# Transposing q by the DMA crossbar instead of by TensorE, from the third batch on

## Chip, cores, metric

One NeuronCore of a Trainium2 chip (trn2). The metric is device time in microseconds of one execution; the kernel before takes 306.1 us.

The profiler's names: PE is TensorE at its matmuls and PEld its weight loads, DVE is VectorE, ACT ScalarE, POOL GpSimd, and SP SyncE, from whose queue (SPq) most DMAs are issued. A crossbar transpose is a DMA that transposes on its way. A transfer lands when its data are there and its semaphore says so. A product or transfer is due when everything ahead of it on its engine is done.

## The reference

Linear attention without softmax, a norm over each head, then a dense layer pair with a quick GELU between.

```python
kv  = np.einsum('bhsd,bhse->bhde', k, v)           # 8 batches, 8 heads, 576 rows, 64 wide
out = np.einsum('bhsd,bhde->bhse', q, kv)
rms = np.sqrt(np.mean(out * out, axis=-1, keepdims=True) + 1e-06)
x   = (out / rms * g_norm)                          # then (b, h, s, d) -> (b s, h d), 4608 x 512
h   = x @ w_in                                      # 512 -> 2048
g   = h * (1.0 / (1.0 + np.exp(-1.702 * h)))
y   = g @ w_out                                     # 2048 -> 512
```

## The kernel before

It runs nine dense layers (one per batch of 512 rows, and a last one for the 8 x 64 rest rows). The attention of batch t + 1 is threaded between the matmuls of layer t. The matmul of this kernel for `out = q kv` takes q with the head dimension on the partitions, so q has to be transposed. The first two batches get this from a matmul with a stacked identity. From the third batch on it is done so:

```python
def q(self, c):                                   # c: pair of heads, 4 per batch
    t = ps_a.tile([P, SM + P], F16, name="qTp", tag="att")
    for j in range(J):                            # 4 transposes of 128x128
        nc.tensor.transpose(t[:, j * P : (j + 1) * P], qh[:, c, j, :], ident)
    n = SM
    if c >= 2:                                    # the rest rows of two pairs
        nc.tensor.transpose(t[:, SM : SM + P], qrem[self.b % 2][:, c - 2, :], ident)
        n += P
    s = attn.tile([P, SM + P], F16, name="qT", tag="qT", bufs=6)
    nc.vector.tensor_copy(s[:, 0:n], t[:, 0:n])   # PSUM to SBUF
    self.qT[c] = s
```

`casts(b)` makes the fp16 copies of k, q and v on DVE, in the order k, q, v for pair 0, then pair 1, and so on. The layers schedule these units by position: `at1(i, ...)` after the i-th of 16 hidden tiles of a layer, `at2(n, ...)` after the n-th of its 64 output matmuls, both counted from 0.

```python
            at1(f0, casts, b)                     # f0 = 7 in the second layer, else 2
            at1(f0, start, b)
            for c in range(NPAIR):
                at1((11 if t == 1 else 8) + c, of(b, "kv", c))
                at1(12 + c, of(b, "q", c))
            for c in range(NPAIR + 1):
                at2(1 + 9 * c, of(b, "out", c))   # first product after output matmul 1
# ... cut
            if b + 2 < B:
                at2(2, load_batch, b + 2)         # and load_batch(3) at the end of the first layer
```

All outputs, the loads of k, q and v from the third batch on and (after the change) the transposes are issued from SP, in program order.

Of the kernel before, what the change touches and what calls it, by code (L numbers as in the profile page):

```python
# [8 lines left out]
F16 = mybir.dt.float16  # L9
# [4 lines left out]
P = 128  # L14
# [3 lines left out]
def kernel(  # L18
# [10 lines left out]
    nc = tc.nc  # L29
# [4 lines left out]
    NPAIR = H // 2  # L34
# [3 lines left out]
    SM = 512  # L38
    J = SM // P
    R = S - SM  # L40
# [7 lines left out]
    attn = ctx.enter_context(tc.tile_pool(name="attn", bufs=4))  # L48
# [3 lines left out]
    ps_a = ctx.enter_context(tc.tile_pool(name="ps_a", bufs=3, space=bass.MemoryType.PSUM))  # L52
# [11 lines left out]
    qrem = [const.tile([P, 2, P], F16, name=f"qrem{i}") for i in range(2)]  # L64
    kbuf = const.tile([P, NPAIR * NJ * P], F16)
    qbuf = const.tile([P, NPAIR * NJ * P], F16)
    vbuf = const.tile([P, NPAIR * NJ * D], F16)
    ident = const.tile([P, P], F16)
# [39 lines left out]
    qh = qbuf[:, 0 : NPAIR * SM].rearrange("p (c j e) -> p c j e", c=NPAIR, j=J)  # L108
# [82 lines left out]
    class Attention:  # L191
# [21 lines left out]
                    r = slice(hl * D, (hl + 1) * D)  # L213
                    nc.vector.tensor_copy(self.kb[r, :, r], t[r, :, r])  # L214

        def q(self, c):
            t = ps_a.tile([P, SM + P], F16, name="qTp", tag="att")
            for j in range(J):
                nc.tensor.transpose(t[:, j * P : (j + 1) * P], qh[:, c, j, :], ident)  # L219
            n = SM  # L220
            if c >= 2:
                nc.tensor.transpose(t[:, SM : SM + P], qrem[self.b % 2][:, c - 2, :], ident)  # L222
                n += P
            s = attn.tile([P, SM + P], F16, name="qT", tag="qT", bufs=6)
            nc.vector.tensor_copy(s[:, 0:n], t[:, 0:n])  # L225
            self.qT[c] = s

        def rest(self, c):
            return self.qT[c | 2][:, SM + (c // 2) * R : SM + (c // 2 + 1) * R]

        def out(self, c):
            t = ps_a.tile([P, NPAIR, P], F32, name="outT", tag="att")
# [52 lines left out]
    class Early(Attention):  # L285
# [17 lines left out]
        def q(self, c):  # L303
            t = ps_h.tile([P, SM], F32, name="q9", tag="hT")
            for j in range(NJ - 1):
                nc.tensor.matmul(
                    t[:, j * R : (j + 1) * R], qz[:, c, j, :], stack, start=True, stop=True
                )
            s = attn.tile([P, SM + P], F16, name="qT", tag="qT", bufs=6)
            nc.vector.tensor_copy(s[:, 0:SM], t)  # L310
            self.qT[c] = s

        def q_rest(self):
# [169 lines left out]
    for t in range(NT):  # L483
        b = t + 1
        u1, u2 = {}, {}

        def at1(i, f, *args):
            u1.setdefault(i, []).append(lambda: f(*args))

        def at2(i, f, *args):  # L490
            u2.setdefault(i, []).append(lambda: f(*args))

        def of(b, name, *args):
            return lambda: getattr(live[b], name)(*args)

        if t == 0:
            at1(("ko", 1), of(0, "ss", NPAIR - 1))
            at1(("ko", 1), of(0, "apply", NPAIR - 1))
            at1(4, of(0, "q_rest"))
            at1(6, of(0, "out", NPAIR))  # L500
            at2(4, of(0, "ss", NPAIR, True))
            at2(4, of(0, "apply", NPAIR))
            at1(8, start, 1)
            for r in krem + vrem:
                at1(8, nc.vector.memset, r[R:P], 0.0)
            for c in range(NPAIR):
                s0 = 14 + 9 * c
                at2(s0 - 6, second_casts, c)
                at2(s0, of(1, "kv", c))
                at2(s0 + 2, of(1, "q", c))  # L510
                at2(s0 + 8, of(1, "out", c))
                at2(s0 + 13, of(1, "ss", c))
                at2(s0 + 13, of(1, "apply", c))
            at2(s0, third)
            at2(63, load_batch, 3)
        elif b < B:
            if t == 1:
                at1(3, of(1, "q_rest"))
                at2(46, of(1, "out", NPAIR))
                at2(53, of(1, "ss", NPAIR))  # L520
                at2(53, of(1, "apply", NPAIR))
            f0 = 7 if t == 1 else 2
            at1(f0, casts, b)
            at1(f0, start, b)
            for c in range(NPAIR):
                at1((11 if t == 1 else 8) + c, of(b, "kv", c))
                at1(12 + c, of(b, "q", c))
            for c in range(NPAIR + 1):
                at2(1 + 9 * c, of(b, "out", c))
                at2(8 + 9 * c, of(b, "ss", c, c == 0))  # L530
                at2(8 + 9 * c, of(b, "apply", c))
            if b + 2 < B:
                at2(2, load_batch, b + 2)
        dense(t, u1, u2, 4 if t < 2 else 0, t == 0)
# [30 lines left out]
```

## Time and profile before

| | before |
|---|---|
| time, median of 3 | 306.1 us (306.08 to 306.12) |
| span of the profiled run | 304.5 us |
| PE busy | 291.9 us, 96% |
| a layer with attention (layers 3 to 7) | 31.8 us |
| a layer without | 27.6 us |

Read it from PE down: where PE has no gap, the length of each piece of PE work is its price. The prediction below shows the stages and the chain. What the q unit does can also be asked by its tile: in the kernel before, this is the view of all instructions that read or write the PSUM tile `qTp` (line, engine, operation, count, then min/median/max ns, and when):

```profile
L219 PE MATMUL qTp<-ident,qbuf x96: 219/219/219, 65.0 to 228.6; 128*128 128x128 f16 x96
L225 DVE COPY qT<-qTp x24: 409/458/493, 65.5 to 228.9; 128x512 f16<-128x512 f16 x12, 128x640 f16<-128x640 f16 x12
L222 PE MATMUL qTp<-ident,qrem x12: 219/219/219, 67.9 to 228.6; 128*128 128x128 f16 x12
```

96 + 12 = 108 transposes and 24 copies are what the change takes away.

### The profile page before, as it was taken

The numbers are of one execution on the slowest core, as the hardware profiler recorded it, in microseconds if no ns is written. First come the engines' busy times: TensorE is split into PE (matmuls) and PEld (weight loads), VectorE is DVE, ScalarE is ACT, GpSimd is POOL, SyncE is SP. The second block draws the span as 40 slices with busy tenths as digits, with TensorE's granted clock in tenths as the row PEclk, the third lists the DMA queues.
The fourth block names the chain that finished last, engine by engine and source line by source line (L and its number), as shares of the span: only waits on it lengthen the run. The fifth ranks groups of instructions, "written<-read, shape, count | busy, mean of one in ns | idle before, by whom it ended". The sixth has DMA issues, their size and how long they took to land.

```text
span 304.5 us, 4193 instructions
## 1 busy us (share of the span) xinstructions
PE 291.9 (96%) x1657; PEld 140.9 (46%) x1657; DVE 108.8 (36%) x225; ACT 183.7 (60%) x293; POOL 29.6 (10%) x52
## 2 busy tenths in 40 slices
PE   6789989999999999999999999999999999999994
PEld 2334454454445544554455444544454444444441
DVE  5651066273461347124523444324523400110021
ACT  7588667757675775667466756585657756007400
POOL 5640070021030100010001000000000000000000
PEclk9999999999999999999999999999999999999999
DMA  6999995999999703870289003000300030002033
GB/s 154 288 176 197 253 262 191 298 334 252 331 237 308 196 0 138 286 182 0 85 276 247 1 0 138 2 0 2 138 0 0 3 138 0 2 15 123 2 69 69
DMA packets 38325, 41.04 MB, mean 135 GB/s; under 512 B 10913, under 2 KB 33441, under 8 KB 37537
## 3 DMA queue, kind: packets, MB, share of 16 engines
q1 hardware_dynamic: 33376, 35.39, 38.8%
q0 software_dynamic: 4768, 5.37, 10.8%
q8 instruction: 13, 0.21, 0.3%
q14 instruction: 8, 0.06, 0.1%
q10 hardware_dynamic: 160, 0.00, 0.0%
HBM read 36.70 MB, written 9.44 MB: 152 GB/s over the span
## 4 chain that ended last, share of the span: by engine, by line
PE 86%; DMA 10%; POOL 1%; SPq 1%; issue 0%; DVE 0%; POOLq 0%
PE o L370 40%; PE hT L329 36%; DMA w_out_sb<-in_moe_w_out_dram 5%; DMA qf<-in_q_dram 3%; PE ss L262 2%; PE outT L234 2%; PE kvp L202 2%; PE qTp L219 2%; DMA kf<-in_k_dram 2%; SPq L93 1%; PE kvp L210 0%; POOL qbuf L101 0%; POOL kbuf L101 0%; PE kv L290 0%; POOL w_in_sb L177 0%
## 5 line engine op out<-in xcount | busy, mean ns | idle before, releaser
L370 PE MATMUL o<-w_out_sb,gT 128*128 128x512 f16 x576 | 137.9, 379 | 0.0
L338 ACT ACTIVATE gT<-hT 128x512 f16<-128x512 f32 x142 | 84.4, 598 | 74.0 <-PE hT L329 73.7
L329 PE MATMUL hT<-xT,w_in_sb 128*128 128x512 f16 x504 | 118.0, 379 | 0.6 <-DVE xT L272 0.5
L370 PEld LDWEIGHTS <-gT 128*128 128x128 f16 x576 | 55.1, 98 | 62.8 <-issue 1.4
L329 PEld LDWEIGHTS <-w_in_sb 128*128 128x128 f16 x576 | 54.5, 98 | 59.8 <-issue 2.2
L378 DVE COPY osb<-o 128x512 f32<-128x512 f32 x34 | 23.3, 684 | 60.8 <-PE o L370 60.8
L272 DVE SCALAR_TENSOR_TENSOR xT<-outT,g_col,rs 128x512 f16<-128x512 f32 x32 | 24.0, 750 | 49.4 <-ACT rs L266 49.4
L264 ACT ACTIVATE ln<-ss,eps_t 128x512 f32<-128x512 f32 (+1 forms) x40 | 25.8, 645 | 18.6 <-PE ss L262 18.5
L266 ACT ACTIVATE rs<-ln 128x512 f32<-128x512 f32 (+1 forms) x40 | 23.5, 587 | 1.3
L254 ACT ACTIVATE sq<-outT 128x512 f16<-128x512 f32 (+1 forms) x40 | 21.6, 541 | 2.7 <-PE outT L234 2.7
L214 DVE CAST kvb<-kvp 64x256 f16<-64x256 f32 x12 | 5.1, 421 | 33.9 <-PE kvp L210 33.8
L145 POOL CAST krem<-krf 64x512 f16<-64x512 f32 x6 | 5.2, 863 | 110.1 <-DMA krf<-in_k_dram 110.1
L225 DVE COPY qT<-qTp 128x512 f16<-128x512 f16 (+1 forms) x24 | 11.0, 457 | 13.4 <-PE qTp L222 8.0
L262 PE MATMUL ss<-sq,ones 128*128 128x512 f16 (+1 forms) x40 | 14.3, 357 | 0.8 <-ACT sq L254 0.6
L329 PE MATMUL hT<-x_rem,w_in_sb 128*128 128x512 f16 x64 | 14.0, 379 | 0.0
L234 PE MATMUL outT<-qT,kvb 128*128 128x512 f16 x32 | 12.1, 379 | 0.5 <-DVE qT L310 0.3
L139 DVE CAST qbuf<-qf 128x512 f16<-128x512 f32 x24 | 10.5, 436 | 2.9 <-DMA qf<-in_q_dram 2.9
L143 DVE CAST vbuf<-vf 128x512 f16<-128x512 f32 x24 | 10.4, 435 | 0.0
L338 ACT ACT_TABLE_LOAD x8 | 10.3, 1283 | 0.1
L276 DVE SCALAR_TENSOR_TENSOR x_rem<-outT,g_col,rs 128x256 f16<-128x256 f32 x8 | 3.9, 483 | 17.9 <-ACT rs L266 17.9
L139 DVE CAST kbuf<-kf 128x512 f16<-128x512 f32 x24 | 10.2, 426 | 0.0
L422 PE MATMUL idle<-kvb 128*128 128x512 f16 x29 | 8.9, 436 | 1.2 <-DVE kvb L160 1.2
(57 smaller groups left out, 142.0 us busy)
## 6 DMA issues: line engine op xcount, KB each, us to landing
kf<-in_k_dram SPq DMA_DIRECT2D x6, 1024.0 KB, 6.8
vf<-in_v_dram SPq DMA_DIRECT2D x6, 1024.0 KB, 10.0
qf<-in_q_dram SPq DMA_DIRECT2D x6, 1024.0 KB, 12.3
out_dram<-osb SPq DMA_DIRECT2D x6, 1024.0 KB, 3.9
kf<-in_k_dram SPq DMA_DIRECT2D x8, 288.0 KB, 6.3
qf<-in_q_dram SPq DMA_DIRECT2D x8, 288.0 KB, 6.1
out_dram<-osb SPq DMA_DIRECT2D x4, 512.0 KB, 5.6
w_in_sb<-in_moe_w_in_dram POOLq DMA_DIRECT2D x2, 512.0 KB, 6.8
```

The source lines that it names most:

```text
L139: nc.vector.tensor_copy(out=dst[:, c, :, :].rearrange("p j (l d) -> p j l d", l=2), in_=src[n][:, h, :].rearrange("p l (j d) -> p j l d", ...
L225: nc.vector.tensor_copy(s[:, 0:n], t[:, 0:n])
L234: nc.tensor.matmul(t.rearrange("p c r -> p (c r)"), self.kb[:, c, :], self.qT[c][:, 0:SM], start=True, stop=True,)
L254: nc.scalar.activation(sq[:, 0:n], t, AFT.Square)
L262: nc.tensor.matmul(t[:, 0:n], ones2, sq[:, 0:n], start=True, stop=True)
L264: nc.scalar.activation(ln[:, 0:n], t[:, 0:n], AFT.Ln, bias=eps_t, scale=1.0 / D)
L266: nc.scalar.activation(rs[:, 0:n], ln[:, 0:n], AFT.Exp, bias=0.0, scale=-0.5)
L272: nc.vector.scalar_tensor_tensor(self.x[:, c, :], o, g_col, rs, op0=ALU.mult, op1=ALU.mult)
L329: nc.tensor.matmul(h, w_in_sb[:, ko, fo * P : (fo + 1) * P], x[:, ko, :], start=(ko == 0), stop=(ko == KO - 1),)
L338: nc.scalar.activation(gT[:, fo, :], h, AFT.Gelu_apprx_sigmoid)
L370: nc.tensor.matmul(os[mo], gT[:, fo, mo * P : (mo + 1) * P], w_out_sb[:, fo, :], start=(fo == 0), stop=(fo == FO - 1),)
L378: (nc.scalar.copy if deep and mo % 2 else nc.vector.tensor_copy)(osb[:, mo, :], os[mo])
```

## The change

Its intent is to take work off PE, which bounds the kernel, and give it to the DMA engines, which stand idle for much of a late layer.

```diff
-        def q(self, c):
-            ...                                   # as above: 4 or 5 TensorE transposes, one PSUM copy
+        def transpose_q(self):
+            s = attn.tile([P, NPAIR * J, P], F16, name="qTd", tag="qTd", bufs=1)
+            nc.sync.dma_start_transpose(out=s, in_=qbuf[:, 0 : NPAIR * SM])
+            self.qTr = attn.tile([P, 2, P], F16, name="qTr", tag="qTr", bufs=1)
+            nc.sync.dma_start_transpose(
+                out=self.qTr, in_=qrem[self.b % 2].rearrange("p c e -> p (c e)")
+            )
+            s = s.rearrange("p (c j) r -> p c (j r)", c=NPAIR)
+            for c in range(NPAIR):
+                self.qT[c] = s[:, c, :]
@@ schedule
-            at2(63, load_batch, 3)                # first layer
             at1(f0, casts, b)
             at1(f0, start, b)
+            at1(f0, of(b, "transpose_q"))
+            if t == 1:
+                at1(f0, load_batch, 3)
             for c in range(NPAIR):
                 at1((11 if t == 1 else 8) + c, of(b, "kv", c))
-                at1(12 + c, of(b, "q", c))
```

(The tile of the first two batches loses its unused tail and two of its six buffers; `rest` reads the new tile.)

More of the change, by code (lines that the diff above doesn't have):

```diff
@@ L214, in kv @@
                     nc.vector.tensor_copy(self.kb[r, :, r], t[r, :, r])
-        def q(self, c):
-            t = ps_a.tile([P, SM + P], F16, name="qTp", tag="att")
-            for j in range(J):
-                nc.tensor.transpose(t[:, j * P : (j + 1) * P], qh[:, c, j, :], ident)
-            n = SM
-            if c >= 2:
-                nc.tensor.transpose(t[:, SM : SM + P], qrem[self.b % 2][:, c - 2, :], ident)
-                n += P
-            s = attn.tile([P, SM + P], F16, name="qT", tag="qT", bufs=6)
-            nc.vector.tensor_copy(s[:, 0:n], t[:, 0:n])
-            self.qT[c] = s
+        def transpose_q(self):
[8 more added lines that the diff above has]
+                self.qT[c] = s[:, c, :]
         def rest(self, c):
-            return self.qT[c | 2][:, SM + (c // 2) * R : SM + (c // 2 + 1) * R]
+            return self.qTr[:, c % 2, (c // 2) * R : (c // 2 + 1) * R]
         def out(self, c):
@@ L308, in q @@
                 )
-            s = attn.tile([P, SM + P], F16, name="qT", tag="qT", bufs=6)
-            nc.vector.tensor_copy(s[:, 0:SM], t)
+            s = attn.tile([P, SM], F16, name="qT", tag="qT", bufs=4)
+            nc.vector.tensor_copy(s, t)
             self.qT[c] = s
```

## The prediction

> **What bounds the kernel now.** I read the page first (busy shares, then the chain that ended last), then the table by stage, then the timeline around the work that the change removes, then the timeline of the DMA queue's own engine.
>
> From the page, the busy shares and the head of the chain:
>
> ```profile
> PE 291.9 (96%) x1657; PEld 140.9 (46%) x1657; DVE 108.8 (36%) x225; ACT 183.7 (60%) x293; POOL 29.6 (10%) x52
> ...
> PE 86%; DMA 10%; POOL 1%; SPq 1%; issue 0%; DVE 0%; POOLq 0%
> ```
>
> PE is busy 96% of the span and makes 86% of the chain; the 10% of DMA lies in the first 38 us, which the change does not touch. From 53 us on, the program is one dense layer per batch, of some 31.8 us, with the attention of the next batch threaded in. The table by stage (PE, PEld, DVE, ACT, POOL busy, then clock, DMA share, GB/s) shows one such layer, from 85.5 us, and one that carries no attention, from 244.6 us:
>
> ```profile
> 85.50:117.30 31.80, 31.80 (x180) 15.62 (x179) 12.66 (x27) 20.91 (x34) 4.37 (x6) 1.00 0.62 158
> ...
> 244.60:272.20 27.60, 27.60 (x130) 12.48 (x129) 2.77 (x4) 9.55 (x16) 0.00 (x0) 1.00 0.10 39
> ```
>
> PE has no gap in either, at clock 1.00. So the price of a piece of PE work is its full length, and all of one batch's attention costs 31.8 - 27.6 = 4.2 us. DVE and ACT have slack.
>
> The q part of that, in the list of the chain in order of time (start, length, what), for the third layer:
>
> ```profile
> 98.03 0.22 PE qTp L219 x4
> 98.25 0.86 PE hT L329 x4
> 99.12 0.22 PE qTp L219 x4
> 99.34 0.86 PE hT L329 x4
> 100.20 0.22 PE qTp L219 x4
> 100.48 0.86 PE hT L329 x4
> 101.35 0.22 PE qTp L219 x4
> 101.62 0.43 PE o L370 x2
> ```
>
> Four transposes take 0.22 us, some 55 ns each in the stream, though one record lasts 219 ns. The third and fourth groups hold a fifth transpose (the rest rows), and take 0.28 and 0.27 us to the next start.
>
> **What the Trainium skill says.** (1) "VectorE: DVE Perf Modes", section The three transpose paths: a 128x128 transpose is 390 ns on TensorE and 1309 ns through the DMA crossbar. The trace agrees that a TensorE transpose is cheap and goes further: in the pipelined stream it costs 55 ns. (2) "Advanced Engine Details and Errata", section X-Bar Transpose (TRN2): crossbar transposes are as fast as regular DMAs, 350 to 400 GB/s expected. (3) "DMA: Bandwidth & Descriptors", section Latency and other measured facts: 261 GB/s measured for a transpose in one kernel. The trace of the kernel before has no transposing DMA, so it confirms neither; its plain loads move about 300 GB/s. (4) The same page, section Queues, rings and completion order: each DMA engine consumes the descriptors of one ring in ring order. The trace fits it: loads issued behind others land later (the 1 MB k, v and q loads of a batch take a median of 6.8, 10.0 and 12.3 us to land, though they are alike).
>
> **The change, part by part.**
>
> Removed from PE: per batch 4 x 4 + 2 = 18 transposes, 0.22 + 0.22 + 0.28 + 0.27 = 0.99 us of the path. Six batches (the third to the eighth): 6 x 0.99 = 5.9 us. All of it is on the path, since PE has no gaps. That is 1.9% of 306.1 us, so even a perfect result stops at 300.2 us, just short of 2%.
>
> Removed from DVE: 24 PSUM copies, the row reads 11.0 us at 457 ns. They lie beside PE work; worth nothing in time. PSUM buffers come free earlier; nothing waited for these.
>
> Added: per batch two DMAs on SP's queue, 128x2048 fp16 (512 KB) and 128x256 (64 KB). Both wait for the fp16 casts; the first product of the batch now waits for the whole big one. Its duration, issue to landing, is the disputed term; call it X. Estimates: 512 KB at the skill's 261 GB/s is 2.0 us, plus what a short DMA takes to land here, 2.3 us (the page's row of 128 KB outputs): 4.3 us. If 16 blocks of 128x128 ran one after another at 1.3 us it would be 21 us. I take X = 5 us, a little over the first[...].
>
> Moved: the load of the fourth batch. It was issued from 56.9 us on, ahead of everything; now it stands on SP behind the first transposes, which wait for the casts.
>
> The window for the transposes is not the same everywhere. In the second layer (first use), in the timeline:
>
> ```profile
> 64.81 0.41 DVE L139 CAST qbuf<-qf 128x512 f16<-128x512 f32 x1
> ...
> 69.64 0.10 PEld L234 LDWEIGHTS <-kvb 128*128 128x128 f16 x1
> ```
>
> The last q cast ends at 65.2; the first product starts at 69.6, or 68.7 once 0.99 us of transposes ahead of it is gone. Window W1 = 3.4 us. Stall S1 = X - 3.4 where positive.
>
> In the third layer the casts end early (about 90.1), but the queue is full. After the first transposes (end 65.3 + X) SP sends the fourth and fifth batches' loads, then the 1.1 MB output of the second layer, then the next transposes. A batch is 3.54 MB, at some 306 GB/s 11.6 us; the output 3.8 us. So those transposes land at 65.3 + X + 11.6 + 11.6 + 3.8 + X = 92.3 + 2X. The need is at 84.7 (layer start less 0.99) + S1 + 14.9 = 99.6 + S1, 14.9 being 100.5 - 85.6 from layer start to first product. Stall S2 = 92.3 + 2X - 99.6 - (X - 3.4) = X - 3.9.
>
> From the fourth layer on the queue is quiet when the casts end: in the timeline of SP the layer's own load starts only after them,
>
> ```profile
> 121.61 0.37 SPq L120 DMA_DIRECT2D kf<-in_k_dram  x1
> 122.28 0.37 SPq L120 DMA_DIRECT2D vf<-in_v_dram  x1
> ```
>
> and it now stands behind the transposes. Casts end 4.6 us after the layer's start, the need is at 14.9: window 10.3 us, no stall unless X is over that. The loads then start X later, but have a whole layer to land.
>
> Sum for X = 5: -5.9 + 1.6 + 1.1 = -3.2, so 302.9 us; I say 303.
>
> **The rivals.** A: the crossbar is as quick as plain DMA (X under 3.5). No stall anywhere, 300.2 us. For it: the skill's rate and the window of 3.4 us; against it: 2.3 us of fixed time leaves 1 us for 512 KB. B: it is about twice slower than I take (X = 8 to 10): S1 + S2 = 2X - 7.3, so 306.1 - 5.9 + 8.7 = 309 to 313 us: the wait on the transpose takes the place of the removed work, and only in two layers. For it: the 1309 ns of a single block, if only partly overlapped. C: blocks go one after another (X about 20): every layer waits, 4 x (20 - 10.3) more, near 370 us. D: the crossbar is not the matter, but the moved load of the fourth batch is: its casts wait at the third layer's start. By the sums above it lands near 65.3 + 5 + 11.6 = 82, before the casts at 86, so I hold it to be hidden unless X passes 9.
>
> **Range and chances.** The floor is 300.2 less a little, so "faster by over 2%" needs more than all the removed PE time: 0.06. X from 3.4 to 9.7 us covers 300.2 to 312.2, "same": 0.75. X above that, or a convoy in the queue: 0.19. The range, 299.8 to 314.0, is X from 0 to about 10.7.
>
> **What would show it.** In the profile after: PE's matmul count down by 108, with no qTp group; q transposes under DMA issues with their landing time, which is X; the first product waiting on that DMA in the second and third layers for about 1.6 and 1.1 us; the layers from the fourth on 30.8 us long instead of 31.8 with no PE idle time. Wrong if X is over 10 us (PE gaps at the first product in every layer), if the transposes hold up SP itself so that loads or outputs come late, or if other loads slow down beside a transpose.

## The result

The changed kernel took 301.24 us (median of 4 runs, 300.47 to 302.05), the kernel before 306.11 us beside it. Ratios here are the mean time of one kernel's fast runs over the mean of the other's fast runs of the same rounds, so they are not quite the ratio of the medians: 0.9841, with a 95% interval of 0.9806 to 0.9876. That is within 2%.

The busy shares and the head of the chain, page of the changed kernel:

```profile
PE 287.3 (96%) x1549; PEld 135.1 (45%) x1549; DVE 98.0 (33%) x201; ACT 184.0 (61%) x293; POOL 28.7 (10%) x52
...
PE 74%; DMA 18%; DVE 3%; POOL 1%; SPq 1%; issue 1%; ACT 0%; POOLq 0%; DVEq 0%
```

PE has 108 matmuls fewer and is 4.6 us less busy; DVE has 24 instructions and 10.8 us less. The chain now goes through DMA for 18% of the span, 8 points more: it passes through the load of the third batch, its casts and the first two transposes. From the chain in order of time (start, length, what):

```profile
49.13 11.93 DMA qf<-in_q_dram
...
65.66 4.39 DMA qTd<-qbuf
...
93.20 8.15 DMA qTd<-qbuf
```

The new operations, from the page's list of DMA issues (the last number is the median time to landing in us; the size of a transpose is not given):

```profile
qTd<-qbuf SPq DMA_TRANSPOSE x6, 4.4
qTr<-qrem SPq DMA_TRANSPOSE x6, 2.7
```

The fourth layer and the one without attention, table by stage:

```profile
117.00:147.81 30.81, 30.81 (x163) 14.65 (x161) 10.84 (x23) 20.64 (x33) 1.51 (x3) 1.00 0.59 169
...
240.23:267.85 27.62, 27.62 (x129) 12.54 (x128) 2.77 (x4) 9.57 (x16) 0.00 (x0) 1.00 0.09 39
```

The fourth to the seventh layer are each 1.0 us shorter and PE still has no gap there. The second and third layers are different. Timeline of the second layer (start, length, engine, what, idle before):

```profile
65.21 0.42 DVE L139 CAST qbuf<-qf 128x512 f16<-128x512 f32 x1
...
65.66 2.01 SPq L218 DMA_TRANSPOSE qTd<-qbuf  x1
...
69.21 0.59 PE L369 MATMUL o<-w_out_sb,gT 128*128 128x512 f16 x2
...
70.09 0.38 PE L233 MATMUL outT<-qTd,kvb 128*128 128x512 f16 x1 [0.29 <-DMA qTd<-qbuf]
```

The two output matmuls take 0.43 us, so the product was due at 69.64 and starts at 70.09: it waits 0.45 us (0.29 of it counted idle, as matmul ends are modelled). In the third layer:

```profile
93.20 6.00 SPq L218 DMA_TRANSPOSE qTd<-qbuf  x1
...
100.69 0.59 PE L369 MATMUL o<-w_out_sb,gT 128*128 128x512 f16 x2
101.40 0.38 PE L233 MATMUL outT<-qTd,kvb 128*128 128x512 f16 x1
```

This transpose is queued behind the fifth batch's load and the second layer's output. It lands 8.2 us after its issue (the longest of the six), and its product waits 0.28 us.

The whole account, from the starts of the layers in both traces: up to the second layer +0.78 us (0.72 of it is there when the first layer starts, as the first loads landed 0.7 us later in this run), second layer -0.55, third -0.72, fourth to seventh -4.01, the rest +0.26 (the last outputs land later). Sum -4.24: span 304.52 to 300.28 us.

### The profile page after: what moved, and what is told of

Its sections match the earlier page's. It is cut to its first block, busy times and chain, and to the rows that moved or that the text cites. A ratio compares the mean times of both kernels' runs of the same rounds, so it can differ in the third digit from the quotient of the medians.

```text
span 300.3 us, 3952 instructions
## 1 busy us (share of the span) xinstructions
PE 287.3 (96%) x1549; PEld 135.1 (45%) x1549; DVE 98.0 (33%) x201; ACT 184.0 (61%) x293; POOL 28.7 (10%) x52
## 4 chain that ended last, share of the span: by engine, by line
PE 74%; DMA 18%; DVE 3%; POOL 1%; SPq 1%; issue 1%; ACT 0%; POOLq 0%; DVEq 0%
PE o L369 37%; PE hT L328 30%; DMA qf<-in_q_dram 7%; DMA w_out_sb<-in_moe_w_out_dram 5%; DMA qTd<-qbuf 4%; PE ss L261 2%; DMA kf<-in_k_dram 2%; PE outT L233 2%; PE kvp L202 1%; SPq L93 1%; DVE qbuf L139 0%; DVE kbuf L139 0%; DVE kbuf L101 0%; DVE vbuf L143 0%; POOL kbuf L101 0%
## 5 line engine op out<-in xcount | busy, mean ns | idle before, releaser
L328 PE MATMUL hT<-xT,w_in_sb 128*128 128x512 f16 x504 | 115.5, 379 | 0.6 <-DVE xT L271 0.5
L328 PEld LDWEIGHTS <-w_in_sb 128*128 128x128 f16 x576 | 55.2, 98 | 63.3 <-issue 2.2
L261 PE MATMUL ss<-sq,ones 128*128 128x512 f16 (+1 forms) x40 | 14.3, 357 | 0.8 <-ACT sq L253 0.6
L145 POOL CAST krem<-krf 64x512 f16<-64x512 f32 x6 | 4.0, 659 | 112.8 <-DMA krf<-in_k_dram 89.4
L421 PE MATMUL idle<-kvb 128*128 128x512 f16 x29 | 10.1, 483 | 1.2 <-DVE kvb L160 1.2
L337 ACT ACT_TABLE_LOAD x8 | 10.3, 1283 | 0.1
L143 DVE CAST vbuf<-vf 128x512 f16<-128x512 f32 x24 | 10.3, 431 | 0.0
L202 PEld LDWEIGHTS <-kbuf 128*128 128x128 f16 x96 | 7.4, 98 | 5.7
L233 PE MATMUL outT<-qTd,kvb 128*128 128x512 f16 x24 | 9.1, 379 | 0.4 <-DMA qTd<-qbuf 0.3
```

Of the source, the lines that this page charges most:

```text
L202: nc.tensor.matmul(t[:, c, :].rearrange("p (l d) -> p l d", l=2), kh[:, c, j, :], vh[:, 2 * c : 2 * c + 2, j * D : (j + 1) * D], start=(j ...
L233: nc.tensor.matmul(t.rearrange("p c r -> p (c r)"), self.kb[:, c, :], self.qT[c][:, 0:SM], start=True, stop=True,)
L261: nc.tensor.matmul(t[:, 0:n], ones2, sq[:, 0:n], start=True, stop=True)
L328: nc.tensor.matmul(h, w_in_sb[:, ko, fo * P : (fo + 1) * P], x[:, ko, :], start=(ko == 0), stop=(ko == KO - 1),)
L337: nc.scalar.activation(gT[:, fo, :], h, AFT.Gelu_apprx_sigmoid)
```

## The experiments

**after_again: the changed kernel once more.** No edit.

> The changed kernel once more, to see whether its times really fall into two groups (300.5 and 302.0 us in the four runs so far, where the kernel before has 306.1 in all) and to get a second trace. Theory A (the two groups come from when the early loads land, before 48 us, and have nothing to do with the transposes): the layers from the fourth on last 30.8 us in any run, and the whole difference between two traces of different groups is there by the start of the second layer (54 us) or in the two first products that wait for a transpose. Theory B (the transposes themselves vary): some layer from the fourth on shows a wait at its first product.

300.66 us (300.51 to 301.31), ratio 0.9829. The profiled run took 300.70 us. In its second layer:

```profile
64.51 1.96 SPq L218 DMA_TRANSPOSE qTd<-qbuf  x1
...
68.34 0.59 PE L369 MATMUL o<-w_out_sb,gT 128*128 128x512 f16 x2
68.91 0.38 PE L233 MATMUL outT<-qTd,kvb 128*128 128x512 f16 x1
```

The product is due at 68.77 and waits 0.14 us; in the third layer 0.15. Layers four to seven take 30.8 us again. Against the first trace, the last copy of an output tile starts 1.33 us earlier: 0.86 of that is there at the start of the second layer, 0.31 and 0.13 are the two waits. So the spread has to do with what happens before 70 us, and with two waits, as theory A had it, except that these waits are for the transposes; no later layer varies. (What sets the longer wait is read from all traces together, at the end of this section.) That the times form two groups was an accident of four runs: with the later ones they fill the stretch from 300.5 to 302.8.

**no_transpose: products read the untransposed copy (wrong result).**

```diff
-            s = attn.tile(...); nc.sync.dma_start_transpose(...)   # both transposes
+            self.qTr = qrem[self.b % 2]
+            for c in range(NPAIR):
+                self.qT[c] = qbuf[:, c * SM : (c + 1) * SM]
```

> All transposes of q taken out: the products read the fp16 copy as it lies (wrong result on purpose). This is the floor: 306.1 - 5.9 = 300.2 us if the removed work is worth what the chain says and nothing else changes. If the two first waits of the changed kernel (0.4 and 0.3 us) are all that the crossbar costs, the changed kernel is 0.7 us above this one in runs with an equal start. If this one lies below 299.5 the crossbar costs more than its visible waits.

300.06 us (299.81 to 300.24), ratio 0.9805. The floor stands where the chain of the kernel before put it. In its trace the first product starts on time:

```profile
68.41 0.59 PE L363 MATMUL o<-w_out_sb,gT 128*128 128x512 f16 x2
68.84 0.38 PE L227 MATMUL outT<-qbuf,kvb 128*128 128x512 f16 x1
```

The changed kernel of the same call is 0.6 us above it. The profiled run of the changed kernel there (300.70 us) has 0.29 us of waits and is 0.46 us above the profiled run of this one (300.24 us). 0.25 us of that lie behind the last layer's start, where PE does the same work and the last outputs land later.

**move_only: the kernel before, with only the load of the fourth batch moved.**

```diff
-            at2(63, load_batch, 3)
             at1(f0, start, b)
+            if t == 1:
+                at1(f0, load_batch, 3)
```

> The kernel before, with only the load of the fourth batch moved behind the casts of the third, as in the changed kernel; q still transposed on TensorE. If the move is hidden (my step D): 306.1 us within 0.3. If the moved load costs, or frees the queue for the first output, 0.5 us or more either way; it may also show the two groups of times, which would then belong to the move and not to the transposes.

305.95 us (305.57 to 306.18), ratio 0.9995: the move by itself costs and gains nothing.

**no_move: the changed kernel with that load back in its old place.** The same two edits, reversed.

> The changed kernel with the load of the fourth batch back in its old place, ahead of the first transposes on the same queue. Theory (transposes stand behind the loads of their queue): the first transposes start behind some 3.5 MB; that load ends near 73 us instead of 65.7, so they land near 74 to 77 us and the first product of the second layer waits 5 to 7 us; the third layer's stall then shrinks to nothing; about 305 to 307 us. Rival (a transpose passes the loads, or the queue is not the limit): no change, 300.5 to 302 us.

312.3 us (311.26 to 312.94), ratio 1.0202. The direction is the theory's; the size is not. SP's timeline and PE's timeline, second layer:

```profile
68.86 3.34 SPq L398 DMA_DIRECT2D out_dram<-osb  x2
72.30 4.71 SPq L218 DMA_TRANSPOSE qTd<-qbuf  x1
```

```profile
78.78 0.59 PE L233 MATMUL outT<-qTd,kvb 128*128 128x512 f16 x1 [10.02 <-DMA qTd<-qbuf]
79.17 3.09 PE L369 MATMUL o<-w_out_sb,gT 128*128 128x512 f16 x7
```

Two things were left out of the 5 to 7 us. SP issues in order and was busy with the load and the first layer's output until 72.2, so the transpose was only issued at 72.3, and its data then stood behind theirs: 6.5 us more. And after the pause of 10 us seven output matmuls took 3.09 us, where they take 1.67 elsewhere in this kernel. The table by stage shows the reason in the clock column:

```profile
78.70:82.00 3.30, 3.22 (x8) 1.13 (x8) 0.00 (x0) 1.88 (x2) 0.00 (x0) 0.50 0.64 197
```

PE ran at half the clock. A wait of 10.2 us (due at 68.6) and some 1.4 us of slow matmuls make 11.6 us in the second layer. The third layer has no wait, as expected. The medians of this kernel and of the changed one beside it are 11.6 us apart; their profiled runs are 11.2 apart, as that of the changed kernel has 0.3 us of waits of its own and starts 0.2 us later.

**late_twice: the large transpose done twice in the fifth to eighth batches.**

```diff
-            nc.sync.dma_start_transpose(out=s, in_=qbuf[:, 0 : NPAIR * SM])
+            for _ in range(2 if self.b >= 4 else 1):
+                nc.sync.dma_start_transpose(out=s, in_=qbuf[:, 0 : NPAIR * SM])
```

> The changed kernel with the large transpose of the fifth to eighth batches done twice, one after the other into the same tile, so that it takes some 2 x 4.4 = 8.8 us there. Theory (a window of 10.3 us in these four layers hides it): no wait, the layers stay at 30.8 us, 300.5 to 302 us. Rival (the crossbar slows PE or other transfers while it runs, or part of it lies on the path already): each of the four layers grows by 0.3 us or more, or by 4.4 if nothing were hidden (318).

301.5 us (300.60 to 302.75), ratio 0.9853. One of the four layers in the table by stage; the other three are 30.80 too:

```profile
141.36:172.16 30.80, 30.80 (x163) 14.65 (x162) 10.83 (x24) 20.60 (x33) 1.51 (x3) 1.00 0.62 169
```

Another crossbar transpose per layer is hidden entirely: the second transpose lands 8.6 to 10.3 us after the issue of the first, and the product is due 10.7 us after it. This run (301.87 us) had the largest waits of all in its second and third layers, where it is the same as the changed kernel: 1.49 and 0.51 us.

**late_thrice: three times.** As above with 3 for 2.

> The same, three times: 3 x 4.4 = 13.2 us, which is 2.9 us over the window of 10.3 us. Theory: each of the four first products of these layers waits 2.9 us for the DMA (a bit less or more as the repeats overlap or not), and the clock may drop a little after it: 301 + 11.6 = 312 to 313 us. If there were no such edge (window larger than reckoned) it stays near 301.

Fast runs 316.09, 317.28 and 320.06 us, ratio 1.0386; the run that was profiled fell in the slow state (341.93 us, clock 0.849). The edge is there, but it costs more than reckoned.

**late_thrice_again: the same kernel.**

> The kernel of late_thrice once more, for a trace in the fast state (its first profile fell in the slow one). Its fast runs took 316 to 320 us, where 312 to 313 were expected. Theory: each of the four first products waits for the DMA for about 3 us, and after that pause PE runs at half clock for some us, as it did after the 10 us wait of no_move (granted clock 0.50 from 78.7 to 82 us), which adds 1 to 1.5 us a layer. Rival: the waits themselves are longer (4 us or more), as the repeats take more than 4.4 us each, and the clock stays at 1.0.

322.4 us, a single run, so its state is unknown; the clock row of its page dips only before the first layer (0.50 from 8.0 to 11.5 us), around the ends of the four waits, and at the very end. The first products of layers four and six:

```profile
135.83 0.59 PE L234 MATMUL outT<-qTd,kvb 128*128 128x512 f16 x1 [3.73 <-DMA qTd<-qbuf]
136.21 3.19 PE L370 MATMUL o<-w_out_sb,gT 128*128 128x512 f16 x7
...
208.77 0.38 PE L234 MATMUL outT<-qTd,kvb 128*128 128x512 f16 x1 [2.10 <-DMA qTd<-qbuf]
208.98 2.74 PE L370 MATMUL o<-w_out_sb,gT 128*128 128x512 f16 x7
```

and the stages right after the first of them:

```profile
135.80:140.00 4.20, 4.17 (x10) 1.47 (x10) 0.00 (x0) 2.01 (x3) 0.00 (x0) 0.50 0.85 256
140.00:142.00 2.00, 2.00 (x8) 0.85 (x7) 0.75 (x1) 1.71 (x3) 0.00 (x0) 0.71 1.10 356
```

The four waits are 3.73, 3.71, 2.10 and 2.09 us, 11.6 us together (as idle time; each is some 0.16 us longer from when the product was due). The sum is what the window of 10.3 us said (4 x 2.9), but no single wait is, so that is luck: one of the three transposes took 5.9 and 6.0 us in layers four and five, where the others took 4.2 to 4.4. Why is not known.

The four layers last 37.20, 37.37, 34.63 and 34.63 us, against 30.80 with two transposes: 20.6 us more. The other 9.0 us are the matmuls at half clock after each wait. By the clock records of the trace the clock was 0.50 for 6.83 us around the end of each of the two long waits and for 3.41 us from the end of each of the two short ones (within 0.7 us); 5.3, 5.7, 3.4 and 3.4 us of that lie behind the waits, and half of their sum is 8.9 us. The theory held in kind, but the slow matmuls cost more than its 1 to 1.5 us a layer; of the rival, two waits came near its 4 us, and its clock of 1.0 fell.

**halves: two transposes of 256 KB into two tiles.**

```diff
-            s = attn.tile([P, NPAIR * J, P], F16, name="qTd", tag="qTd", bufs=1)
-            nc.sync.dma_start_transpose(out=s, in_=qbuf[:, 0 : NPAIR * SM])
+            for h in range(2):
+                s = attn.tile([P, NPAIR * J // 2, P], F16, name=f"qTd{h}", tag=f"qTd{h}", bufs=1)
+                nc.sync.dma_start_transpose(
+                    out=s, in_=qbuf[:, h * NPAIR * SM // 2 : (h + 1) * NPAIR * SM // 2]
+                )
```

> The changed kernel with the large transpose as two of 256 KB into two tiles, so that the first product waits for the first alone. If a transpose's time is a fixed part of some 2.5 us and a rate of some 270 GB/s (from 4.4 us for 512 KB and 2.7 us for 64 KB), the first half lands about 3.4 us after its issue, 1 us sooner than the whole, and the wait in the second layer goes away: 0.1 to 0.4 us less than the changed kernel. If the time is nearly all fixed, the first half takes 4 us or more, and nothing is gained.

300.52 us (300.16 to 301.45), ratio 0.9826. The shortest time to landing is 3.1 us, so a fixed part and a rate describe it, and no product waits in this trace, in the second layer or in the third. The edit does a second thing, which the expectation left out: the first half needs the q casts of two pairs only, and is issued at 63.23 us, 2.2 us before the last q cast ends (65.41). It lands 2.5 us before its product is due (68.84). At 4.4 us in place of 3.1 it would also have landed in time, so this run does not show which of the two took the wait away. The gain on the changed kernel is too small for its spread.

**best: q cast first, and the fifth batch's load behind the third layer's transposes.**

```diff
-        for c in range(NPAIR):                    # k, q, v of pair c
+        for c in range(NPAIR): cast("q", qh, c)   # all q first (written out here)
+        for c in range(NPAIR):
+            cast("k", kh, c); cast("v", vh, c)
@@
-            if t == 1:
-                at1(f0, load_batch, 3)
+            if t < 3:
+                at1(f0, load_batch, t + 2)
@@
-            if b + 2 < B:
+            if b + 2 < B and t > 1:
                 at2(2, load_batch, b + 2)
```

> The changed kernel with both remaining waits addressed: the four q casts come before the k and v casts (the last one ends some 2.4 us sooner), and the fifth batch's load is issued behind the third layer's transposes in place of ahead of them. Theory: both waits (0.1 to 0.4 us, and 0.15 to 0.3 us) go to zero in any run, the third layer's transposes land in 4.4 us in place of 6 to 8, and the time is that of the kernel without transposes, 300.0 to 300.3 us, with less spread than 300.5 to 302. Rival: the k casts, now later, hold up the kv products of the second layer, and it is no better or worse than the changed kernel.

300.69 us (300.15, 300.30, 301.09, 301.25), ratio 0.9827. Its trace, of the 300.15 us run, shows neither wait. Two of its runs are as long as those of the changed kernel, and which of them waited for what is not known. One point of the expectation is wrong: the transposes do not land sooner (6.1 us in the median, up to over 8), as they are now issued while older traffic is still in the queue (from the third layer on, all before the output issued ahead of them has landed; read from the trace, not tested). They are only issued early enough not to matter.

**after_third and best_again: both on one chip, in the same rounds.** No new edit.

> The changed kernel beside best_again on the same chip: 300.5 to 302 us.

> The kernel best once more, beside the changed kernel: no wait at either of the two products (the windows are 2 us or more wider), so it is the faster of the two by the 0.3 to 1.8 us that the trace of each run of the changed kernel shows as waits; its own spread then stems from the early loads alone. If both medians agree within 0.2 us the waits are too small to matter.

The changed kernel: 301.8 us (300.69 to 302.84, 6 runs), ratio 0.9860, interval 0.9840 to 0.9881. best: 300.26 us (300.14 to 300.38, 4 runs), ratio 0.9812, interval 0.9799 to 0.9825. The intervals do not overlap: best is faster by some 0.5%, and beats both kernels. This is on one chip; before, each on another chip and not side by side, best (300.69 us) and after_again (300.66) were alike. How much each of its two edits gave was not separated; in the trace of after_third 1.18 of 1.57 us of waits are in the second layer, where the order of the casts acts. Its second layer:

```profile
62.86 2.31 SPq L226 DMA_TRANSPOSE qTd<-qbuf  x1
...
68.12 0.59 PE L377 MATMUL o<-w_out_sb,gT 128*128 128x512 f16 x2
68.55 0.38 PE L241 MATMUL outT<-qTd,kvb 128*128 128x512 f16 x1
```

The transpose is issued 2.2 us earlier than in the trace of after_third (65.07), and the product starts the moment it is due. The traces side by side, read in the same way (due: start of the two output matmuls plus 0.43 us; move_only and the kernels that wait elsewhere or for longer are left out):

| trace | third batch's q landed | transpose issued, 2nd layer | due | wait, 2nd layer | wait, 3rd layer | time of that run |
|---|---|---|---|---|---|---|
| changed kernel | 61.06 | 65.66 | 69.64 | 0.45 | 0.28 | 302.05 |
| after_again | 59.91 | 64.51 | 68.77 | 0.14 | 0.15 | 300.70 |
| after_third | 60.48 | 65.07 | 68.33 | 1.18 | 0.39 | 301.56 |
| late_twice | 60.96 | 65.55 | 68.49 | 1.49 | 0.51 | 301.87 |
| no_transpose | 60.72 | none | 68.84 | 0 | 0 | 300.24 |
| halves | 60.70 | 63.23 | 68.84 | 0 | 0 | 300.64 |
| best | 59.95 | 62.34 | 68.49 | 0 | 0 | 300.15 |
| best_again | 60.28 | 62.86 | 68.55 | 0 | 0 | 300.21 |

In the first four rows the transpose is issued 4.6 us after that q has landed and takes 4.4 us. So the product starts 9.0 us after the landing, whenever it was due, and the span ends 230.0 to 230.3 us after that product: in these runs the landing of one load sets the time. A wait is what is left between the two moments, and is long where PE comes early. With q cast first the transpose is issued 2.4 to 2.6 us after the landing, and PE comes last again.

The time of each run is also some 300 us plus its waits, within 0.7 us, but for the first row, whose second layer began 0.8 to 1.3 us later than in the other rows. The third batch's load is issued once the last weights have landed, at 47.3, 45.7, 46.9 and 46.6 us in the first four rows, and its q lands 13.6 to 14.3 us after that. Why these moments vary is not known, and no run tested it.

## Why the prediction was right

It said 303.0 us, range 299.8 to 314.0, "within 2%" with a chance of 0.75; measured 301.24. By its own steps:

- **The removed work, 5.9 us.** Right: the kernel without these transposes is at 300.06 us, 6.0 below its neighbour's 306.06, and each of layers four to seven lost 1.0 us. It also set the bound: the best version's ratio is 0.9812, though its interval (0.9799 to 0.9825) just reaches 2%.
- **The copies on DVE, worth nothing.** Consistent: 10.8 us of DVE work went and layers four to seven shrank by no more than the PE work.
- **X, the time of the large transpose.** Guessed 5 us, measured 4.4. The estimate from the skill's 261 GB/s and a short DMA's 2.3 us had given 4.3; the allowance on top of it was not needed. (In the fifth layer it took 6.1 to 6.2 us in each of the three traces of the changed kernel, hidden there; why was not looked for.)
- **The second layer, S1 = X - 3.4.** The mechanism is right. With X = 4.4 it is 1.0 us; the traces show 0.14 to 1.49. What was missed is that the window of 3.4 us is no constant: it is the difference of two moments set by different loads, and varies from run to run. The prediction's 1.6 us was mis-sized by X and by this: from issue to due the window is 2.9 to 4.3 us in the first four rows of the table, and in each of them wait and window add up to 4.4 us, which is X. A smaller slip is in the reading: its line at 69.64 is the weight load, the product itself starts at 69.86, so that the trace of the kernel before gives 3.6 us.
- **The third layer, S2 = X - 3.9.** With X = 4.4 it is 0.5 us; the traces show 0.15 to 0.51. The convoy of loads, output and transpose was reckoned to land at 101.1 us for this X, and landed at 101.4 in the trace. The need was put 0.43 us too early: the 14.9 us lead to the two output matmuls, behind which the product comes.
- **The later layers, window 10.3 us.** Right in kind, shown from both sides: two transposes (8.6 to 10.3 us) are hidden (late_twice), three (12.9 to 14.6 us) are not (late_thrice_again). The window is 10.7 us in both traces, from issue to due; the same 0.43 us was left out.
- **Rival D, the moved load.** Hidden, as held (move_only); in the changed kernel's trace the last big piece of that load lands at 81.5 us, where 82 was reckoned. What the prediction did not say is how much the move is needed: without it the change would have been a loss of 2% (no_move).
- **What it lacked:** a wait on PE was priced at its own length. In the changed kernel the waits are too short for more, but for rivals B and C the price would have been wrong: waits of 2 to 10 us were followed by matmuls at half clock, which in late_thrice_again added 9.0 us to 11.6.

The gap between 303.0 and 301.24 is thus mostly the two waits, 2.7 us reckoned and 0.3 to 2.0 measured. One sum of the range is off: by its own terms 314.0 us stands for X of 10.4, not 10.7, as above 10.3 four more layers wait.

## What to carry to other kernels

Where PE has no gaps, work moved to the DMA engines is gained in full as long as the result is issued early enough, so reckon the window of every use by itself: from the last input's cast to the first consumer, with what stands ahead in the issuing queue. Put urgent short DMAs ahead of bulk loads in that queue, and order the casts so that the DMA's input comes first; the first was worth 11.6 us here (no_move), the second, together with the later load of the fifth batch, 0.5%. And price a wait on PE above some 2 us at more than its length: here the clock fell to 0.50 at waits of 2.09 us and more, and not at 1.32.

## What the Trainium skill lacked or had wrong

- "TensorE: Matmul & The Clock Gate", section Why this matters for your kernels, advises against PE-idle gaps of more than about 3 us. Here gaps of 2.09 and 2.10 us were already followed by slow matmuls (seven in 2.74 us, where 1.67 is usual; granted clock 0.74 from 208 to 211 us, a stretch that includes the end of the gap; by the clock records 0.50 from 209.4 us on, for 3.4 us; a single run of unknown state). The gap of 1.32 us in late_twice was not (seven in 1.67).
- "DMA: Bandwidth & Descriptors", section Latency and other measured facts, gives a rate for transposes but no time for one of middling size. Here: 512 KB in 4.4 us, 256 KB in 3.1 us at best, 64 KB in 2.7 us behind a larger one, and 8.2 us for 512 KB behind loads. Its 261 GB/s with 2.3 us of fixed time fits the 4.4.
- "Advanced Engine Details and Errata", section X-Bar Transpose (TRN2), expects 350 to 400 GB/s. The step from 256 KB (3.1 us at best) to 512 KB (4.3 us at best in the changed kernel) is 1.2 us, some 220 GB/s; a rough figure from two runs.
